# Three four-byte constants take 128 bytes each in SBUF: where the tiles behind them begin, in an attention and two feed-forward layers on one core

## The chip, the cores and the metric

The kernel runs on one core of one Trainium2 chip. The metric is device time in microseconds (us) of one execution, the median of several. A profiled execution gives a trace beside it. A second number, the span, runs from the first to the last instruction of the program in that trace.

## What is computed

The reference, cut to what matters (2 x 12 heads, 448 tokens, 64 columns per head; 896 tokens in all, model width 768, inner width 2048; all float32):

```python
def _attn_ref(q, k, v, cap):
    scores = (1.0 / np.sqrt(q.shape[-1])) * np.matmul(q, k.transpose(0, 1, 3, 2))
    scores = cap * np.tanh(scores / cap)
    attn = np.exp(scores - np.max(scores, axis=-1, keepdims=True))
    attn = attn / (np.sum(attn, axis=-1, keepdims=True) + 1e-09)
    return np.matmul(attn, v)

def _moe_ref(x, w_in, w_out):
    h = x @ w_in
    g = np.where(h >= 1, h, np.where(h <= -1, 0.0, (h + 1) ** 2 / 4))
    return g @ w_out

def _moe2_ref(x, w_in, w_out):
    h = x @ w_in
    return np.maximum(0.01 * h, h) @ w_out
```

The attention's output, 896 tokens by 768, goes through the first feed-forward layer and its result through the second. Where the host's arrays of weights are 64-bit floats, the kernel takes them as pairs of 32-bit words and makes float32 of them itself.

## The kernel before, in words

**The attention** goes through 12 pairs of heads. TensorE (PE) makes the scores of a pair from the tiles `k`, `kl` (last keys) and `q` in plain float32 (L332, L328), ScalarE (ACT) takes tanh and exp into the tiles `e` (L336, L339), PE multiplies them with `v`, `vl` (L347) and sums them with `ones` (L364). Each of these multiplications holds only a part of the PE array, so two or four of them run side by side: four with 32 columns each in L347 and L364. VectorE (DVE) divides and writes the result as two tiles: `xh`, the value rounded to PE's faster 32-bit format (float32r), and `xl`, what the rounding left out.

**The feed-forward layers** multiply in float32r, and each product is made of three: high weights with high values (L237), high weights with what the values' rounding left (L238), low weights with high values (L241). All of that is in `products`. A matmul has a stationary operand, 128 columns of a weight tile `whi` or `wlo`, which a weight load (LDWEIGHTS, shown as the engine PEld) brings into the array before each matmul, and a moving operand, a row of 448 float32 values (1792 bytes) per partition, which then streams through. A layer has two halves of 576 matmuls each:

- the first half (inner width out of model width; 16 weight blocks of 36 matmuls) streams `xh` and `xl`;
- the second half (model width out of inner width; 24 weight blocks of 24 matmuls) streams `gh` and `gl`, the activations of the first half.

So 1152 matmuls stream `xh` or `xl`, 1152 stream `gh` or `gl`, and all 2304 load `whi` or `wlo`.

**A weight block** is loaded from DRAM by the SyncE queue into a raw tile `wr` (L200), made into float32 in a tile `w` by ACT (L223) and DVE (L204, L208, L212, L216), and split into `whi` (ACT, L228) and `wlo` (DVE, L171). There are two `wr`, two `w` and four pairs of `whi` and `wlo`. The activations are made by ACT and DVE out of PSUM (L424 to L431) through three tiles `a`.

**The order of the work** comes from `Plan`: each task has an engine and an estimated cost in a table of formulas, and the planner gives out all instructions in the order of a simulated schedule. No address enters it.

**Where the tiles lie.** Tiles lie in SBUF behind each other in the order in which the kernel asks for them, each in whole units of 32 bytes per partition. The pool `const` holds, in this order, `xh`, `xl`, the three constants `capb`, `rcap` and `half` (L179 to L181, one float32 per partition each), then `wr`, `w`, `whi` and `wlo`. Behind `const` lie the attention's tiles; when the attention is done, the pool `layers` takes their place and holds `gh`, `gl` and `a`. PSUM tiles (`d`) have their own memory.

Of the kernel before, what the change touches and what calls it, by code (L numbers as in the profile page):

```python
# [8 lines left out]
F32 = mybir.dt.float32  # L9
# [115 lines left out]
def tile_softcap_attention_ffn_ffn(  # L125
# [23 lines left out]
    NPAIR, P, _, S = qt.shape  # L149
# [12 lines left out]
    const = ctx.enter_context(tc.tile_pool(name="const", bufs=1))  # L162
# [13 lines left out]

    xh = const.tile([P, KD, NT], F32R, name="xh")
    xl = const.tile([P, KD, NT], F32R, name="xl")
    capb = const.tile([P, 1], F32, name="capb")  # L179
    rcap = const.tile([P, 1], F32, name="rcap")  # L180
    half = const.tile([P, 1], F32, name="half")  # L181

    DS = [ps.tile([P, 2, 512], F32, name=f"d{n}") for n in range(4)]

# [405 lines left out]
```

## Time and profile before

| | us |
|---|---|
| median of three runs | 567.0 |
| lowest and highest of them | 565.86 and 567.14 |
| the profiled execution | 566.49 |
| its span, first to last instruction | 564.7 |

PE is busy 558.3 us of the span, DVE 396.8, ACT 273.3, GpSimd (POOL) 21.4. In the profile a matmul's busy time overlaps with that of the next one, since they are pipelined; how fast they follow each other is read from their starts. The stretches used below are: the end of the first half of layer one (126 to 212 us), its second half (212.2 to 328.9), the first half of layer two (328.9 to 444.2) and its second half (444.2 to 560.7).

### The profile page before, as it was taken

The page shows a single profiled execution, that of the slowest core. Times are in us where ns is not written, and L with a number is a line of the kernel's source. Part 1 is how long each engine was busy: PE and PEld are TensorE (multiplying, and loading weights), DVE is VectorE, ACT ScalarE, POOL GpSimd, SP SyncE. Part 2 cuts the span into 40 slices and gives each one's busy share as a digit, 9 for nine tenths or more (in the row PEclk, how much of TensorE's full clock was granted, in tenths as well). Part 3 has the DMA queues.
Part 4 walks back from the last instruction along what each step waited for, and adds up shares of the span by engine and source line. Part 5 has one row for each costly group of instructions (what it writes and reads, how often), then busy time and mean ns, then how long its engine had stood idle before and what let it go on. Part 6 is the DMA issues. An engine that isn't in the chain of part 4 may idle for free.

```text
span 564.7 us, 7882 instructions
## 1 busy us (share of the span) xinstructions
PE 558.3 (99%) x3031; PEld 463.7 (82%) x3031; DVE 396.8 (70%) x586; ACT 273.3 (48%) x332; POOL 21.4 (4%) x64
## 2 busy tenths in 40 slices
PE   8999999999999999999999999999999999999997
PEld 4332334899999999999999999999999999999996
DVE  2486979849999987756665859988877755646420
ACT  6999998047666655332332335544444432232210
POOL 4221210000000000000000000000000000000000
PEclk9999999999999999999999999999999999999999
DMA  8454653423333323443324333433323144453400
GB/s 223 142 156 139 163 142 94 142 73 112 113 113 115 106 79 95 129 113 111 110 81 156 140 111 114 156 122 113 96 79 107 38 125 132 139 142 93 136 33 34
DMA packets 27622, 65.14 MB, mean 115 GB/s; under 512 B 8384, under 2 KB 14528, under 8 KB 27584
## 3 DMA queue, kind: packets, MB, share of 16 engines
q1 hardware_dynamic: 27328, 64.29, 37.6%
q8 instruction: 24, 0.39, 0.3%
q10 hardware_dynamic: 224, 0.34, 0.2%
q14 instruction: 14, 0.11, 0.1%
q0 software_dynamic: 32, 0.00, 0.0%
HBM read 61.74 MB, written 2.80 MB: 114 GB/s over the span
## 4 chain that ended last, share of the span: by engine, by line
PE 95%; ACT 1%; DMA 1%; DVE 1%; issue 0%; SPq 0%; DVEq 0%; ACTq 0%; POOLq 0%
PE d L237 27%; PE d L241 27%; PE d L238 27%; PE d L347 6%; PE d L332 4%; PE d L364 2%; PE d L328 1%; DMA capb<-cap 1%; ACT e L336 1%; ACT e L339 1%; DMA cs<-xs 0%; DVE t L354 0%; SPq L372 0%; DVE w L212 0%; DVE w L208 0%
## 5 line engine op out<-in xcount | busy, mean ns | idle before, releaser
L237 PE MATMUL d<-gh,whi 128*128 128x448 f32 x384 | 140.3, 365 | 0.0
L238 PE MATMUL d<-gl,whi 128*128 128x448 f32 x384 | 140.2, 365 | 0.0
L237 PE MATMUL d<-xh,whi 128*128 128x448 f32 x384 | 139.5, 363 | 0.0
L238 PE MATMUL d<-xl,whi 128*128 128x448 f32 x384 | 139.2, 362 | 0.0
L228 ACT CAST whi<-w 128x512 fp32r<-128x512 f32 (+1 forms) x80 | 56.4, 705 | 137.7 <-PE d L238 89.3
L241 PE MATMUL d<-xh,wlo 128*128 128x448 f32 x384 | 111.9, 362 | 0.0
L241 PE MATMUL d<-gh,wlo 128*128 128x448 f32 x384 | 111.7, 365 | 0.0
L171 DVE TENSOR_TENSOR wlo<-w,whi 128x512 fp32r<-128x512 f32 (+1 forms) x80 | 63.4, 792 | 54.3 <-ACT whi L228 54.2
L237 PEld LDWEIGHTS d<-xh,whi 128*128 128x128 f32 x384 | 72.1, 188 | 6.5 <-DVE xs L380 0.7
L241 PEld LDWEIGHTS d<-gh,wlo 128*128 128x128 f32 x384 | 72.1, 188 | 5.7
L237 PEld LDWEIGHTS d<-gh,whi 128*128 128x128 f32 x384 | 72.1, 188 | 5.7
L238 PEld LDWEIGHTS d<-gl,whi 128*128 128x128 f32 x384 | 72.1, 188 | 5.7
L241 PEld LDWEIGHTS d<-xh,wlo 128*128 128x128 f32 x384 | 72.1, 188 | 4.7
L238 PEld LDWEIGHTS d<-xl,whi 128*128 128x128 f32 x384 | 72.1, 188 | 4.7
L223 ACT ACTIVATE w<-wr 128x512 f32<-128x512 f32 (+1 forms) x80 | 61.4, 767 | 16.2 <-DVE wlo L171 6.7
L212 DVE SCALAR_TENSOR_TENSOR w<-wr,w 128x512 int32<-128x512 int32 (+1 forms) x80 | 63.9, 798 | 2.4
L216 DVE SCALAR_TENSOR_TENSOR w<-wr,w 128x512 int32<-128x512 int32 (+1 forms) x80 | 63.8, 797 | 2.4
L429 DVE TENSOR_TENSOR a<-d,a 128x896 f32<-128x896 f32 x32 | 34.7, 1086 | 16.2 <-ACT a L428 15.8
L336 ACT ACTIVATE e<-d,rcap 128x896 f32<-128x896 f32 (+1 forms) x48 | 41.4, 909 | 7.2 <-PE d L332 3.9
L208 DVE TENSOR_SCALAR w<-w 128x512 int32<-128x512 int32 (+1 forms) x80 | 38.5, 481 | 2.7
L204 DVE TENSOR_SCALAR w<-w 128x512 f32<-128x512 f32 (+1 forms) x80 | 37.7, 472 | 3.5 <-ACT w L223 3.5
L339 ACT ACTIVATE e<-e,capb 128x1792 f32<-128x1792 f32 (+1 forms) x24 | 38.5, 1603 | 0.8
(48 smaller groups left out, 373.8 us busy)
## 6 DMA issues: line engine op xcount, KB each, us to landing
wr<-w1o SPq DMA_DIRECT2D x24, 512.0 KB, 3.6
wr<-w2i SPq DMA_DIRECT2D x16, 768.0 KB, 4.3
wr<-w2o SPq DMA_DIRECT2D x24, 512.0 KB, 3.7
wr<-w1i SPq DMA_DIRECT2D x11, 768.0 KB, 4.3
wr<-w1i SPq DMA_DIRECT2D x15, 256.0 KB, 3.2
v<-vt SPq DMA_DIRECT2D x12, 256.0 KB, 3.3
bc<-rr SPq DMA_DIRECT2D x24, 112.0 KB, 4.0
out<-a SPq DMA_DIRECT2D x12, 224.0 KB, 4.3
```

The lines of the kernel that those rows point to most:

```text
L171: nc.vector.tensor_tensor(out=out_, in0=x, in1=f32(hi), op=ALU.subtract)
L204: nc.vector.tensor_scalar(out=f32(w), in0=f32(w), scalar1=W_MIN, scalar2=W_MAX, op0=ALU.max, op1=ALU.min)
L208: nc.vector.tensor_scalar(out=w, in0=w, scalar1=3, scalar2=LOW_30, op0=ALU.logical_shift_left, op1=ALU.bitwise_and)
L212: nc.vector.scalar_tensor_tensor(out=w, in0=r[:, :, 1], scalar=SIGN_AND_TOP, in1=w, op0=ALU.bitwise_and, op1=ALU.bitwise_or)
L216: nc.vector.scalar_tensor_tensor(out=w, in0=r[:, :, 0], scalar=29, in1=w, op0=ALU.logical_shift_right, op1=ALU.bitwise_or)
L223: add("ACT", act(n) + 0.06, lambda: nc.scalar.activation(f32(w), f32(r[:, :, 1]), AF.Abs), R, [W])
L228: add("ACT", act(n), lambda: nc.scalar.copy(h, f32(w)), [W], [H])
L237: nc.tensor.matmul(o[:, b, :S], ch, h[:, f, r], start=first, stop=False)
L238: nc.tensor.matmul(o[:, b, :S], ch, l[:, f, r], start=False, stop=False)
L241: nc.tensor.matmul(o[:, b, :S], cl, h[:, f, r], start=False, stop=last)
L336: add("ACT", act(n * S, 1), lambda: nc.scalar.activation(e, d[:, :n, :S], AF.Tanh, scale=rcap), [("d", t % 2)], [key])
L339: add("ACT", act((2 + n) * S, 1), lambda: nc.scalar.activation(whole, whole, AF.Exp, scale=capb), [], [key])
```

## The change

The three constants become the first columns of tiles of 32 float32 values. Nothing else is edited; a line fewer stands ahead of the rest of the kernel, so its lines from L182 on count one less.

```diff
     xh = const.tile([P, KD, NT], F32R, name="xh")
     xl = const.tile([P, KD, NT], F32R, name="xl")
-    capb = const.tile([P, 1], F32, name="capb")
-    rcap = const.tile([P, 1], F32, name="rcap")
-    half = const.tile([P, 1], F32, name="half")
+
+    capb, rcap, half = (x[:, :1] for x in [const.tile([P, 32], F32, name=n) for n in ("capb", "rcap", "half")])
```

The instructions, their order on every engine and their tiles' names are the same in both programs. What differs are addresses. First bytes within a partition, as the two programs are built, and what is left of them over a multiple of 128:

| tile | before | over | after | over |
|---|---|---|---|---|
| `xh` | 16512 | 0 | 16512 | 0 |
| `xl` | 38016 | 0 | 38016 | 0 |
| `capb` | 59520 | 0 | 59520 | 0 |
| `rcap` | 59552 | 32 | 59648 | 0 |
| `half` | 59584 | 64 | 59776 | 0 |
| `wr`, first of two | 59616 | 96 | 59904 | 0 |
| `w`, first of two | 71904 | 96 | 72192 | 0 |
| `whi`, first of four | 78048 | 96 | 78336 | 0 |
| `wlo`, first of four | 81120 | 96 | 81408 | 0 |
| `q`, first of three | 102624 | 96 | 102912 | 0 |
| `k`, first of three | 108000 | 96 | 108288 | 0 |
| `e`, first of four | 122976 | 96 | 123264 | 0 |
| `gh` | 102624 | 96 | 102912 | 0 |
| `gl` | 159968 | 96 | 160256 | 0 |
| `a`, first of three | 217312 | 96 | 217600 | 0 |

The rows of `xh`, `xl`, `gh` and `gl` that a matmul streams lie 1792 bytes apart, and the 128 columns of weights that it loads 512 bytes apart; both are multiples of 128, so every operand of a layer's matmul has its tile's remainder. Of the smaller tiles behind `const` (`cs`, `rc`: 56 and 28 bytes) some begin between multiples of 128 in both programs.

## Rows read from the trace of the kernel before

**Rows 1.** Page, part 1: busy us, share of the span, instructions.

```profile
PE 558.3 (99%) x3031; PEld 463.7 (82%) x3031; DVE 396.8 (70%) x586; ACT 273.3 (48%) x332; POOL 21.4 (4%) x64
```

**Rows 2.** Page, part 4: the chain that ended last, by engine.

```profile
PE 95%; ACT 1%; DMA 1%; DVE 1%; issue 0%; SPq 0%; DVEq 0%; ACTq 0%; POOLq 0%
```

**Rows 3.** Windows: length, busy us and count by engine, clock, DMA.

```profile
126.00:211.90 85.90, 85.90 (x431) 80.62 (x430) 83.01 (x110) 56.27 (x68) 0.00 (x0) 1.00 0.32 105
212.20:328.70 116.50, 116.50 (x576) 107.97 (x575) 77.33 (x125) 36.41 (x55) 0.00 (x0) 1.00 0.39 120
328.90:444.00 115.10, 115.10 (x577) 108.01 (x577) 95.45 (x120) 54.62 (x66) 0.00 (x0) 1.00 0.33 104
444.20:560.70 116.50, 116.50 (x577) 107.98 (x575) 56.91 (x99) 31.81 (x53) 0.00 (x0) 1.00 0.35 102
```

**Rows 4.** Timeline at the borders of stretches: start, length, engine, line, instruction.

```profile
212.20 0.37 PE L237 MATMUL d<-gh,whi 128*128 128x448 f32 x1
...
328.93 0.37 PE L237 MATMUL d<-xh,whi 128*128 128x448 f32 x1
...
444.16 0.37 PE L237 MATMUL d<-gh,whi 128*128 128x448 f32 x1
...
560.70 0.37 PE L241 MATMUL d<-gh,wlo 128*128 128x448 f32 x1
```

**Rows 5.** Lines of PE in stretches two and three: count, busy us, mean ns.

```profile
L237 PE MATMUL d<-gh,whi 128*128 128x448 f32 x192 | 70.1, 365 | 0.0
...
L237 PE MATMUL d<-xh,whi 128*128 128x448 f32 x192 | 69.6, 363 | 0.0
```

**Rows 6.** Lines of the weight loads: count, busy us, mean ns, idle before.

```profile
L237 PEld LDWEIGHTS d<-gh,whi 128*128 128x128 f32 x384 | 72.1, 188 | 5.7
...
L237 PEld LDWEIGHTS d<-xh,whi 128*128 128x128 f32 x384 | 72.1, 188 | 6.5 <-DVE xs L380 0.7 <-issue 0.7 <-DVE a L429 0.3
...
L347 PEld LDWEIGHTS d<-e,vl 128*32 128x32 f32 x96 | 3.1, 110 | 5.9 <-issue 5.4 <-POOL kl L310 0.5
```

**Rows 7.** Timeline of PE in the third stretch.

```profile
429.96 0.36 PE L238 MATMUL d<-xl,whi 128*128 128x448 f32 x1
429.97 0.19 PEld L237 LDWEIGHTS d<-xh,whi 128*128 128x128 f32 x1
430.16 0.36 PE L237 MATMUL d<-xh,whi 128*128 128x448 f32 x1
430.17 0.19 PEld L238 LDWEIGHTS d<-xl,whi 128*128 128x128 f32 x1
430.36 0.36 PE L238 MATMUL d<-xl,whi 128*128 128x448 f32 x1
```

**Rows 8.** Timeline of PE in the attention stage.

```profile
51.51 0.93 PE L347 MATMUL d<-e,vl 128*32 128x448 f32 x8
...
52.26 0.55 PE L364 MATMUL d<-t,ones 128*32 128x448 f32 x2
```

**Rows 9.** Lines of DVE and ACT, whole span.

```profile
L429 DVE TENSOR_TENSOR a<-d,a 128x896 f32<-128x896 f32 x32 | 34.7, 1086 | 16.2 <-ACT a L428 15.8 <-ACT a L426 0.2
L171 DVE TENSOR_TENSOR gl<-a,gh 128x896 fp32r<-128x896 f32 x32 | 34.7, 1086 | 1.7 <-ACT gh L431 0.8
...
L171 DVE TENSOR_TENSOR xl<-d,xh 128x896 fp32r<-128x896 f32 x6 | 6.5, 1092 | 18.4 <-ACT xh L458 18.4
```

**Rows 10.** Waits, whole span: us in total, times, longest.

```profile
ACT whi L228 <- PE d L238: 89.3, 30, 4.2
...
ACT w L223 <- DMA wr<-w1i: 5.0, 1, 5.0
...
DVE rcap L296 <- DMA capb<-cap: 4.6, 1, 4.6
...
PEld d L332 <- DMA k<-kt: 0.5, 1, 0.5
```

**Rows 11.** Waits of the DMA queue SP, whole span.

```profile
SPq L200 <- DVE w L216: 383.7, 73, 15.9
```

**Rows 12.** Page, part 6: DMA issues, KB each, us to landing.

```profile
wr<-w2i SPq DMA_DIRECT2D x16, 768.0 KB, 4.3
```

## The prediction

> **What bounds the kernel now.** I began with the page's first part and its chain of waits. PE is busy 99% of the span [rows 1] and makes up 95% of the chain that ended last [rows 2], so only what changes PE's pace, or keeps PE waiting, can move the time. The windows by stretch say that PE never pauses in the layers: in each of the four stretches its busy time is the stretch's length, at a granted clock of 1.00, the 2.4 GHz level [rows 3]. DVE comes near it in one place only, the end of the first layer's first half, with 83.0 us of 85.9 [rows 3].
>
> A busy PE may still not be PE at its best, so I took the pace from the starts. The second half of layer one begins at 212.20 and the first half of layer two at 328.93 [rows 4]: 576 matmuls in 116.73 us, 202.65 ns each. The next half, to 444.16, takes 115.23 us [rows 4], 200.05 ns each. The last half has its last matmul at 560.70 [rows 4]: 575 steps in 116.54 us, 202.68 ns each. All three have the same shape (192 matmuls for each of the three lines, 128x448 [rows 5]) and no wait, yet the halves that stream `gh` and `gl` are 2.6 ns a matmul slower than the one that streams `xh` and `xl`. The mean lengths agree: 365 ns against 363 [rows 5]. In the table of addresses these two pairs differ in just the thing that the change edits: `xh` and `xl` begin at multiples of 128, `gh` and `gl` 96 bytes past one. So the trace of before holds half of the experiment already.
>
> Why 200 ns at all? At 2.4 GHz 448 columns, one per clock, would be 186.7 ns. The rows of the third stretch show a circle: a load of weights starts with the matmul ahead of it (429.97 behind 429.96), takes 188 ns [rows 6], and the matmul it serves starts at 430.16 [rows 7]; the next load starts with that one. Load and start-up together make 200 ns, so with an aligned moving operand the loads set the pace, and the stream, shorter, hides in it. With the operand at 96 the load is still 188 ns [rows 6], so what grew past 200 ns must be the stream. A row of 1792 bytes covers 14 stretches of 128 bytes when it begins on one, and 15 when it begins 96 bytes in. If PE fetches such stretches and a whole one costs its 32 columns, 15 take 480 clocks, 200.0 ns. The attention gives the rest: two rounds of four matmuls lie between 51.51 and 52.26 [rows 8], 375 ns a round, against 373.3 ns for 448 columns at two clocks each; about 2 ns per matmul are not streaming. 200.0 and 2 are 202, near the 202.7 measured; 14 stretches give 189, below the circle of 200.
>
> **The change, part by part.**
>
> *The moving operand of the second halves.* `gh` and `gl` go from 96 to 0, which is where `xh` and `xl` are now. 1152 matmuls fall from 202.67 to 200.05 ns: 1152 x 2.62 = 3.0 us less. All of it lies on the path, since PE has no wait there. By the fall to the stream alone (189 ns) it would be more, but the circle of loads stops it at 200.05. The lower bound of this term is nothing (the two halves differ for another reason).
>
> *The stationary operand of all 2304 matmuls.* `whi` and `wlo` go from 96 to 0 as well, and no row of before shows a load from a multiple of 128, so this is bounded from both sides. A load of 32 columns takes 110 ns and one of 128 takes 188 [rows 6], 0.81 ns a column on top of some 84 ns that do not depend on the number. At 96 bytes in, a load of 512 bytes touches five stretches instead of four. If the fifth costs nothing, the pace stays 200.05. If a load waits for the 8 columns (32 bytes) of the broken first stretch, it would lose 8 x 0.81 = 6.5 ns when aligned; if a fifth stretch costs as much as 32 columns, 26 ns. In the last case the circle is shorter than the stream and the pace is 186.7 ns or a little more. I take nothing. The reason is the attention: there a column takes two clocks, its tiles too begin 96 bytes in, and the round is within 2 ns of pure streaming [rows 8], so at half pace the broken stretch is hidden. A load, with its 0.81 ns (two clocks) a column, is nearest to that row. A cost above today's is not excluded, and stands as a rival below.
>
> *The attention's tiles.* A round can gain at most the 2 ns above streaming; nine groups of two rounds for each of 12 pairs are 216 rounds, 0.4 us at most. I take nothing.
>
> *DVE and ACT.* DVE's subtraction of 896 columns takes 1086 ns where all its tiles are at 96 (`gl`), and 1092 ns where it writes the aligned `xl` from PSUM [rows 9]; the maximum out of PSUM into `a` takes 1086 too. No price of alignment shows, I take zero. Were there one, the cover is wide: ACT waits 89.3 us in all for PE to free weight tiles [rows 10]. Only at the end of the first half of layer one is it thin, 2.9 us.
>
> *DMA.* A weight block lands in 4.3 us [rows 12]; its queue waits 383.7 us for DVE to free `wr` [rows 11], and ACT's longest wait for a block is 5.0 us once [rows 10], while PE's own weight loads wait just 0.5 us for a transfer, at the start. A tenth of a landing either way, 0.4 us, is hidden by the 89.3 us above; without this cover it would cost 0.4 us for each of 80 blocks at most, 34 us, but that would need every block to be late. The transfer of `capb`, waited for 4.6 us [rows 10] at the start, goes to the same address as before.
>
> **The sum.** The profiled execution took 566.49 us, 0.5 below the median of 567.0 of the runs. From it 3.0 come off, 563.5; the same step from the median gives **564.0 us**, my forecast, and with 0.5 to either side for the unpriced small terms, 563.2 to 564.8.
>
> **The rivals.**
>
> *The loads get shorter too.* For it: the load is what sets the pace of 200 ns, and it has never been seen aligned. Against it: the row at half pace above. With the 6.5 ns of a broken first stretch the pace is 193.5 everywhere: 1152 x 9.1 + 1152 x 6.5 = 18.0 us less, 549 us. DVE would just follow (2.8 us less in the end of the first half, where it has 2.9). With 26 ns the stream binds at 186.7: 1152 x 16.0 + 1152 x 13.4 = 33.8, of which DVE holds back about 2.9, some 536 us.
>
> *Alignment is nothing to PE.* The two halves may differ for a reason I don't see (what is in the tiles, which addresses they have beyond the remainder). Then nothing moves: 567 us. [...]
>
> *It is the difference that counts.* `xh` and `xl` at 0 meet weights at 96; `gh` and `gl` at 96 meet weights at 96. If loads and streams get in each other's way when both begin at the same remainder, it is now the first halves that are free of it, and after the change no half is: all operands are at 0. Then 1152 matmuls go from 200.05 to 202.67, 3.0 us more, **570.0 us**, slower. It decides once equal remainders cost the first halves more than 1.5 ns a matmul (1.7 us over 1152), while the second halves, equal before and after, gain nothing. Against it: the load has 188 ns in both kinds of halves [rows 6], and two streams in each other's way should show in both. [...]
>
> That the change does not do what it says I leave aside: the built addresses show that it does.
>
> **How the numbers follow.** The forecast gets 0.48: the two paces are measured, on 576 matmuls each, and the 128-byte account gives both to a nanosecond. Shorter loads get 0.20, of which two thirds near 549 and a third deeper. No effect gets 0.20, the difference 0.12. About 0.3% or 1.7 us is what a measurement of this kernel can tell from no change. Faster by more than that: the loads' 0.20 and nearly all of the forecast, 0.66. Within it: 0.22, the rest of the forecast with the second rival. Slower: 0.12. The range must reach over no change, 567 with a little for the runs' own spread, and down to the nearer loads' case: 548 to 568. It leaves out the slower rival and the deep end of the loads, 0.19 together. The likeliest case has 563.2 to 564.8.
>
> **What would show it.** Right: the starts that bound the second halves lie 115.2 us apart instead of 116.7, the mean of a `gh` matmul falls from 365 to 363 ns, the first halves keep their 115.2, loads keep 188 ns. Shorter loads: the mean of 188 falls, and the first halves get shorter as well. No effect: all stretches as before. The difference: the first halves go to 116.7. What would make me wrong in another way is a wait of PE inside a layer that is not there now.

## The result: 571.2 us, slower, and the profile after

The changed kernel takes **571.17 us**, the median of 7 runs (570.71 to 575.59), against 566.95 for the kernel before. The ratio is 1.0092, with a 95% interval from 1.0064 to 1.012: slower by 4.2 us, or 0.9%, where 3.0 us less was forecast. The profiled execution is the longest of the seven, 575.59 us; a second trace of the same kernel (run a2_again below) has 571.24 us, which is typical. Medians below are of all executions of a kernel, and ratios leave out those that lie more than 1.5% above its shortest.

The starts at the borders of the stretches, from the timeline of the profiled execution after (the same four starts as in [rows 4]; lines count one less):

```profile
216.78 0.36 PE L236 MATMUL d<-gh,whi 128*128 128x448 f32 x1
...
335.81 0.36 PE L236 MATMUL d<-xh,whi 128*128 128x448 f32 x1
...
453.31 0.36 PE L236 MATMUL d<-gh,whi 128*128 128x448 f32 x1
...
569.84 0.36 PE L240 MATMUL d<-gh,wlo 128*128 128x448 f32 x1
```

The first half of layer two, between the second row and the third, takes 117.50 us where it took 115.23: 204.0 ns a matmul instead of 200.05. Its `xh` and `xl` have not moved by a byte; only its weights have. The last half (575 steps to its last matmul) takes 116.53 us, 202.7 ns, as before; the second half of layer one 119.03, which is 206.6 ns with the same addresses. The second trace has the same first halves, and the second half of layer one at its old pace:

```profile
214.69 0.37 PE L236 MATMUL d<-gh,whi 128*128 128x448 f32 x1
...
331.44 0.36 PE L236 MATMUL d<-xh,whi 128*128 128x448 f32 x1
...
448.94 0.37 PE L236 MATMUL d<-gh,whi 128*128 128x448 f32 x1
...
565.49 0.37 PE L240 MATMUL d<-gh,wlo 128*128 128x448 f32 x1
```

116.75, 117.50 and 116.55 us, that is 202.7, 204.0 and 202.7 ns. Of the 4.8 us between the spans (569.5 against 564.7) the two first halves make up 2.2 and 2.3, the start of the layers 0.3 (92.89 instead of 92.56). The first trace is 4.4 us longer than the second by the 206.6 ns (2.3 us) and by a late attention: its layers begin at 94.98 us instead of 92.89. This was lost at the start of the attention, in the first matmuls of the scores. Two rows of the first trace:

```profile
4.30 5.72 PE L331 MATMUL d<-q,k 64*128 64x448 f32 x12
...
5.79 0.50 PEld L331 LDWEIGHTS d<-q,k 64*128 64x128 f32 x4 [0.99 <-DMA q<-qt]
```

And one of the second:

```profile
4.30 2.76 PE L331 MATMUL d<-q,k 64*128 64x448 f32 x8
```

In the first trace the first twelve are done at 10.02 us, in the second at 8.33. One weight load waits 0.99 us for a transfer of `q` there, and the twelve matmuls are longer, 951 ns in the median against 658. The scores of the last keys then begin at 10.33 us instead of 8.30, and the 2.0 us between them stay to the end of the attention. Why that execution began so is open.

The groups of the page after that answer to [rows 5, 6 and 9], with mean lengths in ns:

```profile
L236 PE MATMUL d<-xh,whi 128*128 128x448 f32 x384 | 140.8, 367 | 0.0
...
L236 PE MATMUL d<-gh,whi 128*128 128x448 f32 x384 | 140.8, 367 | 0.0
...
L236 PEld LDWEIGHTS d<-xh,whi 128*128 128x128 f32 x384 | 72.1, 188 | 7.8 <-DVE xs L379 0.7 <-issue 0.7 <-DVE a L428 0.2
...
L428 DVE TENSOR_TENSOR a<-d,a 128x896 f32<-128x896 f32 x32 | 34.7, 1087 | 18.5 <-ACT a L427 18.1 <-ACT a L425 0.2
```

A matmul on `xh` went from 363 to 367 ns, the load of weights kept its 188, and DVE's maximum its 1086 or 1087. The mean on `gh`, 367 ns, mixes the half at 206.6 ns with the one at 202.7.

### The profile page after: what moved, and what is told of

Its sections match the earlier page's. It is cut to its first block, busy times and chain, and to the rows that moved or that the text cites. A ratio compares the mean times of both kernels' runs of the same rounds, so it can differ in the third digit from the quotient of the medians.

```text
span 573.8 us, 7882 instructions
## 1 busy us (share of the span) xinstructions
PE 567.0 (99%) x3031; PEld 463.7 (81%) x3031; DVE 397.2 (69%) x586; ACT 273.3 (48%) x332; POOL 20.9 (4%) x64
## 4 chain that ended last, share of the span: by engine, by line
PE 95%; DVE 1%; SPq 1%; DMA 1%; ACT 1%; issue 0%
PE d L236 27%; PE d L240 27%; PE d L237 27%; PE d L346 5%; PE d L331 5%; PE d L327 1%; PE d L363 1%; DMA bc<-rr 1%; PE d L283 1%; SPq L371 0%; ACT e L338 0%; DVE t L353 0%; SPq L386 0%; SPq L273 0%; ACT e L335 0%
## 5 line engine op out<-in xcount | busy, mean ns | idle before, releaser
L240 PE MATMUL d<-xh,wlo 128*128 128x448 f32 x384 | 113.3, 366 | 0.0
L428 DVE TENSOR_TENSOR a<-d,a 128x896 f32<-128x896 f32 x32 | 34.7, 1087 | 18.5 <-ACT a L427 18.1
```

The source lines that it names most:

```text
L240: nc.tensor.matmul(o[:, b, :S], cl, h[:, f, r], start=False, stop=last)
```

## The experiments

I will call **distance** what is left of (first byte of the weights minus first byte of the moving operand) over a multiple of 256. The table of addresses gives remainders over 128; over 256, `xh` and `xl` lie at 128 in both kernels, the weights, `gh` and `gl` at 224 before and at 0 after. So the distance was 96 in the first halves and 0 in the second; after the change it is 128 and 0.

**1. The pace at 32 pairs of starts (m1_offsets).** PE alone, in place of the whole kernel; `stat` holds the four tiles of weights, `mov` the eight moving rows, N is 60:

```diff
+    for y in stat:
+        for x in mov:
+            w, m = stat[y].bitcast(F32R), mov[x].bitcast(F32R)
+            for n in range(N):
+                b = (0, 0, 1, 1, 0, 1)[n % 6]
+                nc.tensor.matmul(d[:, b, :S], w, m, start=n in (0, 2), stop=n >= N - 2)
```

> This kernel leaves out the attention and both layers: PE only runs 32 series of 60 float32r matmuls of 448 columns, each with its own weight load, the weights beginning 0, 32, 64 or 96 bytes past a multiple of 256 (tiles wa to wd) and the moving row 160, 192, 224, 0, 32, 64, 96 or 128 past one (tiles ma to mh); it writes a constant. Theory D (the distance from the moving operand's start to the weights' start sets the pace): the pace of a series depends on weights minus moving alone, in bytes over a multiple of 128 or 256. A distance of 96, that of the first halves before, gives 200 ns; 0 and 128, those of all halves after the change, 202.7 to 206.7 ns; series of the same distance agree whatever the two starts are. Theory S (weights that begin at a multiple of 128 are slow to load or in the way): all series of wa stand at 204 ns or more and those of wd do not, whatever the moving row. Theory M (the moving operand's own start, as in the prediction): ma and me, mb and mf and so on agree for all four weights, and md and mh are at 200.

The timeline of PE puts a series into one row: start, length, tiles. The pace is the step to the start of the next series, over 60.

```profile
41.31 12.56 PE L39 MATMUL d<-md,wa 128*128 128x448 f32 x60
53.71 12.43 PE L39 MATMUL d<-me,wa 128*128 128x448 f32 x60
65.98 12.17 PE L39 MATMUL d<-mf,wa 128*128 128x448 f32 x60
77.98 12.48 PE L39 MATMUL d<-mg,wa 128*128 128x448 f32 x60
90.30 12.40 PE L39 MATMUL d<-mh,wa 128*128 128x448 f32 x60
102.54 12.40 PE L39 MATMUL d<-ma,wb 128*128 128x448 f32 x60
114.78 12.18 PE L39 MATMUL d<-mb,wb 128*128 128x448 f32 x60
...
151.18 12.56 PE L39 MATMUL d<-me,wb 128*128 128x448 f32 x60
163.58 12.43 PE L39 MATMUL d<-mf,wb 128*128 128x448 f32 x60
...
224.72 12.55 PE L39 MATMUL d<-mc,wc 128*128 128x448 f32 x60
237.11 12.29 PE L39 MATMUL d<-md,wc 128*128 128x448 f32 x60
...
334.73 12.18 PE L39 MATMUL d<-md,wd 128*128 128x448 f32 x60
346.75 12.29 PE L39 MATMUL d<-me,wd 128*128 128x448 f32 x60
```

For the weights at 0 (`wa`), `md` (also at 0; distance 0) has 12.40 us to the next start, 206.7 ns; `mf`, at 64 (distance 192), 12.00 us, 200.0; `mh`, at 128, 12.24 us, 204.0. With other weights the same distance has the same pace: `ma` on `wb`, 160 and 32, is distance 128 again and has 12.24 us; `me` on `wb`, both at 32, 206.7. Of the 32 series 30 can be read: `ma` on `wa` opens the run, with 249.7 ns and a slow beginning, and the last has no series behind it. In seven of the eight groups of one distance all series agree within 0.3 ns, whatever the two starts are, which leaves theory D and takes away S and M. One group is split: at distance 96, `mc` on `wc` has 12.39 us, 206.5 ns, while `md` on `wd` has 12.02, 200.3, and `mb` on `wb` 200.3 as well.

**2. All four halves at distance 96 (e1_g_as_x, e2_weights_at_0).** The first is the kernel before with only `gh` and `gl` moved:

```diff
                 pool = ctx.enter_context(tc.tile_pool(name="layers", bufs=1))
+                pool.tile([P, 40], F32, name="ahead")
```

The second is the changed kernel; it leaves the weights where the change puts them and moves the four operands:

```diff
+    const.tile([P, 8], F32, name="ahead")
     xh = const.tile([P, KD, NT], F32R, name="xh")
...
-    capb, rcap, half = (x[:, :1] for x in [const.tile([P, 32], F32, name=n) for n in ("capb", "rcap", "half")])
+    capb, rcap, half = (x[:, :1] for x in [const.tile([P, k], F32, name=n) for n, k in (("capb", 32), ("rcap", 32), ("half", 24))])
...
                 pool = ctx.enter_context(tc.tile_pool(name="layers", bufs=1))
+                pool.tile([P, 40], F32, name="front")
```

> The kernel before with 160 bytes ahead of gh and gl, so that these begin 128 past a multiple of 256, as xh and xl do, and the weights stay at 224: the distance is 96 in all four halves. Theory D: the second halves run at 200.05 ns like the first, 3.0 us less, 564 us. Theory S: the weights are where they were and so is the time, 567 us, unless the moving operand's start counts as well (theory M: 564 too).

> The changed kernel, with 32 bytes ahead of xh and 160 ahead of gh: the weights stay at multiples of 256, and all four moving tiles begin 160 past one, 32 past a multiple of 128; the distance is 96 in all four halves. Theory D: all halves at 200.05 ns, 564 us, as in the run with gh moved alone. Theory S: first halves at 204 ns as after the change, and the second at 202.7 or more, 570 us or more. Theory M (a moving operand away from a multiple of 128 is slow): 202.7 or more in all halves, 570 us or more.

564.55 us and 564.28 us; the ratios to the kernel before are 0.9952 (0.9933 to 0.9971) and 0.9947 (0.9928 to 0.9966). The borders of e1:

```profile
212.86 0.36 PE L237 MATMUL d<-gh,whi 128*128 128x448 f32 x1
...
328.06 0.36 PE L237 MATMUL d<-xh,whi 128*128 128x448 f32 x1
...
443.26 0.36 PE L237 MATMUL d<-gh,whi 128*128 128x448 f32 x1
...
558.26 0.36 PE L241 MATMUL d<-gh,wlo 128*128 128x448 f32 x1
```

115.20, 115.20 and 115.00 us: 200.0 ns everywhere. In the trace of e2 the second half of layer one begins at 213.16 us of a span of 562.6, which leaves 349.4 us as here (212.86 of 562.3): the same pace. So weights at a multiple of 256 are not slow there, and rows 32 bytes past a multiple of 128 are not either. What counts is how the two lie to each other.

**3. Which halves lost (e3_g_only, e5_x_only).** The changed kernel, with one pair of moving operands put to distance 96. In e3 these are `gh` and `gl`:

```diff
                 pool = ctx.enter_context(tc.tile_pool(name="layers", bufs=1))
+                pool.tile([P, 40], F32, name="ahead")
```

In e5 they are `xh` and `xl`; its edit is that of e2 without the 160 bytes (`front`) ahead of `gh`.

> The changed kernel with 160 bytes ahead of gh and gl only: the distance is 128 in the first halves, as after the change, and 96 in the second. Theory D: 204.0 ns in the first halves, 200.0 in the second, 3.0 us less than the changed kernel where its second halves run at 202.7: 568.2 us, and with 1152 x 4.0 = 4.6 us of first halves still above the 564.3 of the two runs with 96 throughout. If the first halves were not what made the change slow, this run would be at 564 to 565.

> The changed kernel with 32 bytes ahead of xh and 32 fewer in half's tile, so that weights and gh and gl stay as after the change (distance 0 in the second halves) and the first halves have distance 96. Theory D: first halves at 200.0 ns, 1152 x 4.0 = 4.6 us below the changed kernel, 566.6 us, if the second halves run at 202.7 as in the kernel before; each second half at 206.7 adds 2.3. If the loss were not in the first halves, 571 us.

e3 took 572.52 us, ratio 1.0093 (1.0058 to 1.0127), not the 568.2 expected; its four executions lie between 572.19 and 574.11. The borders of the profiled one say why:

```profile
215.17 0.36 PE L236 MATMUL d<-gh,whi 128*128 128x448 f32 x1
...
334.20 0.36 PE L236 MATMUL d<-xh,whi 128*128 128x448 f32 x1
...
451.69 0.37 PE L236 MATMUL d<-gh,whi 128*128 128x448 f32 x1
...
566.70 0.36 PE L240 MATMUL d<-gh,wlo 128*128 128x448 f32 x1
```

The second half of layer one took 119.03 us: distance 96, but 206.7 ns, the second pace that one series had shown. The first half of layer two has 204.0 (117.49 us), the last half 200.0 (115.01). 576 x 6.65 ns is 3.8 us above expectation, of 4.3 that were missing. So the first halves' loss is there, and a distance does not give one pace for sure. e5 took 568.42 us, the median of five executions. Four of them, 566.09 to 569.49 us, lie between the 566.6 expected and the 571 of a loss that is elsewhere, and spread too much to show more. The fifth is the profiled one, 581.5 us, with all its halves at 206.7 ns: from 218.86 us to the end of its span it has 360.8 us where e1 has 349.4, 6.6 ns more for each of 1728 matmuls, and ahead of that 432 matmuls fall into 89.0 us where 431 fell into 85.9 [rows 3]; this trace therefore can't show the 200.0 that it was made for.

**4. Finer steps, and one series behind another (m2_fine, a2_again).**

```diff
+    for i, x in enumerate("abcdefghijklmnop"):
+        t = pool.tile([P, S + 64], F32, name=f"m{x}")
+        mov[x] = t[:, i * 4:i * 4 + S]
...
+    for x in "iabcdefghijklmnopkakiaikea":
```

Run a2_again is the changed kernel without any edit.

> This kernel leaves out the attention and both layers: 26 series of 96 float32r matmuls with one tile of weights at a multiple of 256 and moving rows 0 to 240 bytes past one in steps of 16 (tiles ma to mp, in order, after a first series of mi), and then again mk, ma, mk, mi, ma, mi, mk, me, ma, that is distances 96, 0, 96, 128, 0, 128, 96, 192, 0 one behind the other; it writes a constant. Theory D: the series at multiples of 32 repeat the first table, and the steps of 16 lie on or between their neighbours; a distance with less than 200 ns would show that the circle of loads is not the floor. Two paces: distance 0 at 206.7 behind one neighbour and 202.7 behind another; if it is 206.7 each time, the 202.7 of the layers has another reason, such as the weights' tile that changes there with each triple.

> The changed kernel once more, for a second trace, since in its first one the second half of layer one ran at 206.6 ns and that of layer two at 202.7 with the same addresses. Theory D with two paces: first halves (distance 128) at 204.0 ns again in both; second halves (distance 0) each at 202.7 or at 206.7, and at 571 us rather both at 202.7. If 206.6 in layer one belongs to that layer (its loads, its other engines), it comes again.

The paces by distance, from the starts of m1 and m2, in ns:

| distance | 0 | 16 | 32 | 48 | 64 | 80 | 96 | 112 |
|---|---|---|---|---|---|---|---|---|
| pace | 202.7 or 206.6 | 202.6 | 204.3 | 204.0 | 202.2 | 204.3 | 200.2 or 206.6 | 206.6 |

| distance | 128 | 144 | 160 | 176 | 192 | 208 | 224 | 240 |
|---|---|---|---|---|---|---|---|---|
| pace | 204.0 | 206.7 | 205.3 | 203.3 | **200.1** | 202.9 | 204.5 or 206.6 | 202.2 |

At 448 columns none of these 16 distances has less than 200 ns. The steps of 16 do not all lie between their neighbours, as was expected: 80, 112 and 144 lie above the lower paces of both. Each odd multiple of 16 ran in one series only, so whether it has a second pace is open.

Eight of the last nine series of m2, in the timeline of PE (the very last has no series behind it):

```profile
344.53 19.37 PE L35 MATMUL d<-mk,w 128*128 128x448 f32 x96
363.74 19.62 PE L35 MATMUL d<-ma,w 128*128 128x448 f32 x96
383.20 19.39 PE L35 MATMUL d<-mk,w 128*128 128x448 f32 x96
402.43 19.74 PE L35 MATMUL d<-mi,w 128*128 128x448 f32 x96
422.01 19.63 PE L35 MATMUL d<-ma,w 128*128 128x448 f32 x96
441.48 19.74 PE L35 MATMUL d<-mi,w 128*128 128x448 f32 x96
461.06 19.99 PE L35 MATMUL d<-mk,w 128*128 128x448 f32 x96
480.89 19.37 PE L35 MATMUL d<-me,w 128*128 128x448 f32 x96
```

`mk`, distance 96, takes 19.21 and 19.23 us (200.1 and 200.3 ns) where it comes at 344.53 and 383.20, and 19.83 us (206.6) at 461.06, with the same tiles. `ma`, distance 0, takes 19.46, 19.47 and, earlier, 19.83 us. The same instructions on the same addresses have two paces: the means of whole series of `mk` are 200.1, 200.1, 200.3 and 206.6 ns, and none lies between. Behind `mi`, `ma` ran at 202.8 here and at 206.6 at the start of the run, so the neighbour alone does not choose. The a2 trace, shown above, has it in the kernel: 206.6 does not belong to layer one.

**5. How long the row is (m3_lengths).** Rows of 512, 448, 384 and 256 columns at the distances 128, 96, 192 and 0:

```diff
+    for x, at in ("i", 32), ("k", 40), ("e", 16), ("a", 0):
+        for y, cols in ("p", 512), ("q", 448), ("r", 384), ("s", 256):
+            t = pool.tile([P, 512 + 64], F32, name=f"m{x}{y}")
+            mov[x + y] = t[:, at:at + cols]
```

> This kernel leaves out the attention and both layers: 17 series of 96 float32r matmuls, with moving rows of 512, 448, 384 and 256 columns (last letter p, q, r, s) that begin 128, 160, 64 or 0 past a multiple of 256 (i, k, e, a; distances 128, 96, 192, 0), weights at 0, after a first series of miq; it writes a constant. Theory C (the circle of load and start sets 200 ns, the stream hides in it): 384 and 256 columns run at 200 ns, at the distances 96 and 192 and with less stream to be in the way at the others too, and 512 columns at 213 to 216 ns where the stream is free. Theory N (each load takes slots of 16 columns, 6.67 ns, from the stream, two of them at best): 512 columns run at 226.7 ns at 96 and 192, 384 columns at 173 to 175 or at a floor that the load sets below 200; the price of the bad distances over the best is the same 2 to 7 ns at 512 columns.

```profile
103.21 22.65 PE L36 MATMUL d<-mkp,w 128*128 128x512 f32 x96
125.70 19.38 PE L36 MATMUL d<-mkq,w 128*128 128x448 f32 x96
...
172.94 22.13 PE L36 MATMUL d<-mep,w 128*128 128x512 f32 x96
194.91 19.36 PE L36 MATMUL d<-meq,w 128*128 128x448 f32 x96
214.11 16.80 PE L36 MATMUL d<-mer,w 128*128 128x384 f32 x96
230.75 11.47 PE L36 MATMUL d<-mes,w 128*128 128x256 f32 x96
242.06 21.95 PE L36 MATMUL d<-map,w 128*128 128x512 f32 x96
263.84 19.62 PE L36 MATMUL d<-maq,w 128*128 128x448 f32 x96
```

At distance 192 (`me`), 384 columns take 16.64 us for 96 matmuls, 173.3 ns, and 256 columns 11.31 us, 117.8; at distance 0 (`ma`), 512 columns take 21.78 us, 226.9. Theory C is gone: with 384 and 256 columns the pace goes far below 200. The loads keep their mean of 188 ns at 384 columns, so that at a pace of 173.3 they overlap each other. From 384 columns to 448 the best pace grows by 26.7 ns, 0.417 ns a column. At that price 384 columns are 160.0 ns and 448 are 186.7, and 13.3 ns stand on top of both, near theory N's two slots of 6.67. 512 columns would be 213.3 + 13.3 = 226.7, near the 226.9; at 256 columns less stands on top, 117.8 over 106.7. Theory N missed where the best pace lies: it expected 226.7 for 512 columns at 96 and 192, and they took 22.49 us, 234.3 ns, at 96 and 21.97 us, 228.9, at 192. The best distance differs with the length.

**6. Another distance with the best pace (e4_192, e4b_192, e1b_96).** All moving operands 64 past a multiple of 256, the weights on one:

```diff
+    const.tile([P, 48], F32, name="ahead")
     xh = const.tile([P, KD, NT], F32R, name="xh")
...
-    capb, rcap, half = (x[:, :1] for x in [const.tile([P, 32], F32, name=n) for n in ("capb", "rcap", "half")])
+    capb, rcap, half = (x[:, :1] for x in [const.tile([P, 16], F32, name=n) for n in ("capb", "rcap", "half")])
...
                 pool = ctx.enter_context(tc.tile_pool(name="layers", bufs=1))
+                pool.tile([P, 16], F32, name="front")
```

Run e4b_192 is e4 once more, run e1b_96 is e1 once more.

> The changed kernel with the weights at multiples of 256 and all four moving tiles 64 past one: a distance of 192 in all halves, by the series of matmuls the one other distance with 200.0 ns. Theory D: 200.0 in all halves, 564.3 us, the same as with 96. If the runs at 96 owe some of their spread to a second pace (one of four series at 96 ran at 206.7), this one spreads less; a theory in which 96 is special (the moving operand 32 bytes past a multiple of 128, or the weights at 96) has it at 570 or more.

> Distance 192 in all halves once more, beside distance 96 on one chip. In all series and halves so far 192 had one pace, 200.0 ns; 96, 0 and 224 had a second one, 206.7 ns, into which they fell or not. If that is so, no run of this kernel takes longer by the price of a half at the second pace (576 x 6.7 = 3.8 us and more, up to four halves, 15 us): all runs at 563 to 567 us. If the second pace is something else's (the chip's, the data's), it shows at 192 as well.

> Distance 96 in all halves once more. With the second pace: most runs at 563 to 566 us, some longer by 3.8 us for each half that falls into it, up to 579 us. If it has one pace only, all runs lie as close together as those at 192.

e4 took **563.81 us**, ratio 0.9943 (0.9922 to 0.9963), and in its second turn 564.62, 0.9953 (0.993 to 0.9975); its 16 runs lie between 562.90 and 566.43. Borders of e4:

```profile
212.48 0.36 PE L237 MATMUL d<-gh,whi 128*128 128x448 f32 x1
...
327.68 0.36 PE L237 MATMUL d<-xh,whi 128*128 128x448 f32 x1
...
442.88 0.36 PE L237 MATMUL d<-gh,whi 128*128 128x448 f32 x1
...
557.88 0.37 PE L241 MATMUL d<-gh,wlo 128*128 128x448 f32 x1
```

115.20, 115.20 and 115.00 us, 200.0 ns. At distance 96 the second turn has a median of 565.39 us over six executions; two of these took 578.72 and 578.79 us, and without them the ratio is 0.9953 (0.9925 to 0.9981). The first of the two is the profiled one, and it is in the second pace, at the same granted clock of 1.00:

```profile
216.03 0.37 PE L237 MATMUL d<-gh,whi 128*128 128x448 f32 x1
...
335.07 0.37 PE L237 MATMUL d<-xh,whi 128*128 128x448 f32 x1
...
454.11 0.37 PE L237 MATMUL d<-gh,whi 128*128 128x448 f32 x1
...
572.95 0.36 PE L241 MATMUL d<-gh,wlo 128*128 128x448 f32 x1
```

119.04, 119.04 and 118.84 us: 206.7 ns in all of them. No run at 192 had it, and no series of 448 columns at 192. That is what 16 runs show, not a proof that it can't be.

Other kernels had such long executions too: e1 one of 11 (578.38 us), e2 one of 9 (579.80), and the kernel before 10 of the 59 that were taken beside all these runs, 577.58 to 581.18 us. With all four halves at 206.7 ns the kernel before would take 1152 x 6.65 + 1152 x 4.0 = 12.3 us more than its 566.5, that is 578.8. So the second pace is the likely reason, but none of those was profiled. In all four halves it costs three times what the change does.

## Why the prediction was wrong

**What bounds the kernel** was read rightly: PE has no wait in the layers after the change either (busy 121.0 us of 121.0 from 95 to 216 us, and 352.4 of 352.4 in the three halves behind), and in the second trace all of the loss but the 0.3 us of a later start lies in its pace there. The **two paces** of before, 202.7 and 200.05, were right too, and that an address was behind them.

**The step that failed** is the one from there to the moving operand: "with an aligned moving operand the loads set the pace, and the stream, shorter, hides in it". There is no circle of 200 ns: with 384 columns the pace is 173.3 ns, with loads of the same 188 ns. The 2.4 GHz of the prediction, 186.7 ns for 448 columns at one per clock, no row of before shows; the 0.417 ns a column of run m3 makes the same number. The start of a load at the start of the matmul ahead of it, [rows 7], is true, but at 384 columns the loads follow each other every 173.3 ns all the same. And what made 2.6 ns of difference was not the 15th stretch of 128 bytes but the distance between two operands, 96 in the one kind of half and 0 in the other: the rows of e2, 32 bytes past a multiple of 128, cover 15 too and run at 200.0 ns. The account agreed with both numbers to a nanosecond, and it had been fitted to just these two.

**The moving operand's term**, 3.0 us less, was nothing: `gh` and `gl` moved by 288 bytes together with their weights, so their distance stayed 0 and their pace 202.7 (a2), or 206.6 in one half of the first trace.

**The stationary operand's term** I had bounded by nothing on the side of a loss, and left the loss to a rival. It was the result: 1152 x (204.0 - 200.05) is 4.6 us, where the two first halves of the second trace lost 2.2 and 2.3 and the medians lie 4.2 apart. The reason for nothing, that a load is nearest to the attention's row at half pace, did not carry over. Runs e1 and e2 against each other show that moving the weights costs nothing as long as the operands follow.

**The rival that named the distance** was right that the difference of the two starts counts, and near in its time, 570.0 against 571.17. Mis-sized was its price: I gave equal remainders over 128 the 2.6 ns of distance 0, but what counts repeats at 256, not at 128: 64 and 192 have 202.2 and 200.1 ns. After the change the distance is 128, which costs 4.0 ns. My argument against it, that "two streams in each other's way should show in both", did not hold: with rows of 448 columns the loads' mean is 187 or 188 ns at the distances 0, 96, 128 and 192 alike (before, after, e4 and m3), and only the pace changes, 200.0 ns at 192 and 204.0 at 128.

**The rival of shorter loads** did not come: a load has 188 ns from a multiple of 256 as it had before.

**The rival of no effect** did not come: the first halves went from 200.05 to 204.0 ns by the weights' new addresses alone, and in steps of 16 bytes the paces go from 200.1 to 206.7 ns.

**The terms of zero** held. DVE's 896 columns take 1087 ns at the new addresses, the attention ends 0.3 us later in the second trace (2.4 us in the first, by its slow beginning), and DMA never came into the layers' path: the one weight load that waits for a transfer, 0.99 us, is at the start of the attention.

What the runs show is that the pace follows the difference of the two starts, over 256 (200.1 to 206.7 ns at 448 columns), and the row's length (117.8 ns at 256 columns, 228.9 at 512, both at distance 192). What makes it so was not shown, since no run leaves the loads out, and what picks one of two paces stays open. Distances that differ between high and low parts were not tried.

## What to carry to other kernels

Where PE bounds a kernel and each matmul brings its own load, look at where the weights begin relative to the moving row, not at whether either is aligned: here 160 bytes ahead of two tiles gave 0.5%, and rounding every tile to 128 bytes lost 0.9%. The search is cheap, a kernel of matmuls alone with a series for each pair of starts, and a pace read from starts of series in the timeline; a matmul's own length, 361 to 367 ns here, overlaps with the next one and is not its pace. Run the candidates often enough to see whether they have a second pace: 96 and 192 have the same ratio here, and only 96 had executions of 579 us. An explanation that fits two numbers and has been made from them is to be tried on a third, such as another row length, before a forecast rests on it.

## What was not expected of the hardware

- From 384 to 448 columns the best pace of a float32r matmul with its own load of 128 columns grows by 0.417 ns a column (173.3 and 200.0 ns), with 13.3 ns on top of the columns at that price, about as much for 512 (226.9), and some 20 ns at a bad distance (206.7 for 448, 234.3 for 512).
- Distances 0, 96 and 224 have two paces, 202.7, 200.0 or 204.5 ns and 206.7, for the same matmuls. At 96 an execution whose last three halves are in the second one took 578.72 us, one with all three at 200.0 took 564.04, at granted clocks of 1.000 and 0.999.
